# The first part of an attention-and-MoE kernel as one list of one-engine steps

## The chip, the cores and the metric

The kernel runs on one core of one Trainium2 chip. The metric is device time in microseconds (us), the median of several executions; one more execution is profiled. PE is the matmul engine (PEld its weight loads), DVE is VectorE, ACT is ScalarE, POOL is GpSimd, SP only issues DMAs.

## What is computed

```python
scores = scale * (q_c @ k_c.T)              # 8 batches, 8 heads, chunks of 64 tokens, head size 64
attn = softmax(scores)                      # max, exp, sum, divide
x = (attn @ v_c), laid out as 4608 tokens x 512
h = max(max(x @ w1, x @ w2), x @ w3)        # three 512 x 768 weights
x = h @ w_out                               # 768 x 512
h = maximum(x @ w_in2, 0) ; out = h * h @ w_out2    # 512 x 2048, 2048 x 512
```

q, k and v are float32; all weights arrive as float64.

## The kernel before, in words

Attention works on 36 tiles of 128 tokens; four tiles make a block of 512 tokens, so there are nine blocks. A matmul operand is kept as two float32r parts, a high part and the low rest, and every product is three matmuls (high-high, high-low, low-high) of 128x256.

A tile passes through S (scores, on PE), the row maximum and the subtraction (DVE, L277 and L280), the exponential (ACT, L281), the row sum and its reciprocal (DVE, L287 to L292), the product with the reciprocal (POOL, L293), T (transpose, PE), a copy out of PSUM (ACT, L303), X (the product with v, PE), the high part (ACT, L328) and the low part (DVE, L333).

A float64 weight tile of 128x512 is called a unit; there are 24 in the first part (w1, w2, w3 and w_out for each of six slices f of 128 hidden columns). `convert` turns one into its two parts: ACT takes the absolute value of the upper words and the scaled lower words (L98, L99), DVE rebuilds the exponent in three steps (L101, L103, L106), POOL adds the lower words (L112), ACT rounds to the high part (L113), POOL subtracts for the low part (L115). Raw tiles go through four buffers (`in`).

An item (b, f, w) is the projection of block b with weight w of slice f: 24 matmuls into one of two PSUM buffers (`p`). w = 0 is copied out by ACT (L375), w = 1 and w = 2 take the running maximum on DVE (L378, L382), and after w = 2 ACT and DVE make the two parts of h (L384, L386). `g2(b, f)` multiplies them by w_out, also 24 matmuls, into four accumulators. At the end of block 0 these are written out.

The first part runs under a manual schedule: each engine gets its instructions in the order in which the Python code emits them. It covers eight attention tiles (blocks 0 and 1), the 24 conversions, all 36 items of blocks 0 and 1, the products `g2` of block 0, and the scores and the transposes of tiles 8 and 9 and the scores of 10 and 11. A loop over the eight tiles interleaves attention, conversion and the first items; a second loop takes the other items, and a generator `flow` works off the conversions from unit 8 on, mostly one after the other. `heat(n)` emits n matmuls on zeros. After the first part come the products of block 1, the other blocks and the second MoE layer, whose code is not touched; they begin with X of tiles 8 and 9.

Of the kernel before, what the change touches and what calls it, by code (L numbers as in the profile page):

```python
# [2 lines left out]

# [38 lines left out]
def kernel(ctx: ExitStack, tc, qkv, w123, w_out, w_in2, w_out2, out):  # L42
# [48 lines left out]
    def convert(raw, hi, lo):  # L91

        w0, w1 = raw[:, :, 0], raw[:, :, 1]
        a = tmp("a")
        r = tmp("r")
        au, ru = a.bitcast(U32), r.bitcast(U32)
        v = nc.vector
        nc.scalar.activation(a, w1.bitcast(F32), AF.Abs)  # L98
        nc.scalar.activation(ru, w0, AF.Copy, scale=2.0**-29)  # L99
# [6 lines left out]
        v.scalar_tensor_tensor(out=au, in0=w1, scalar=0xC0000000, in1=au, op0=ALU.bitwise_and, op1=ALU.bitwise_or)  # L106
        if hi is None:
            for h, part in enumerate(lo):
                c = slice(h * HC, h * HC + HC)
                nc.gpsimd.tensor_tensor(out=part.bitcast(U32), in0=au[:, c], in1=ru[:, c], op=ALU.add)  # L110
            return
# [5 lines left out]
    def unit_steps(src, name, keep, late=False):  # L117
# [7 lines left out]
        if src.dtype == F32:  # L125
            raw = ap.tile([P, 512], F32, tag="in", name="raw", bufs=4)
            nc.sync.dma_start(raw, src)
            yield
            split(halved(raw), hi, lo)
        else:  # L130
            raw = ap.tile([P, 512, 2], U32, tag="in", name="raw", bufs=4)
            nc.sync.dma_start(raw.rearrange("p n w -> p (n w)"), src.bitcast(U32))
            yield
            yield from convert(raw, hi, lo)

# [37 lines left out]
    def park(n, g):  # L173
# [5 lines left out]
        for r in range(2):  # L179
            for a in range(2):  # L180
# [5 lines left out]
                else:  # L186
# [3 lines left out]
                    for k, _ in enumerate(convert(raw, None, parts)):  # L190
                        if k in (0, 2):
                            yield
# [81 lines left out]
    def att_M(t):  # L274
# [5 lines left out]
        nc.vector.tensor_tensor(out=e, in0=s, in1=mx.to_broadcast([P, H, D]), op=ALU.subtract)  # L280
        nc.scalar.activation(e, e, AF.Exp, scale=1.0 / D ** 0.5)  # L281
        e_t[t] = e

    def att_N(t):
# [21 lines left out]
    def att_V(*ts, tag="at"):  # L306
# [19 lines left out]
        for t in ts:  # L326
            o = t % 4
            nc.scalar.copy(x_t[t // 4][0][:, :, o * P:o * P + P], xps_t[t])  # L328
# [42 lines left out]
    def p1_end(b, f, w, p):  # L371
# [181 lines left out]
    for f in range(NF1):  # L553
        units += [w123_steps(f, w) for w in range(3)] + [wo_steps(f)]
# [16 lines left out]
    M = [att_M(t) for t in range(8)]  # L571
    N = [att_N(t) for t in range(8)]
    U = units
    none = iter(())

    heat(11)
    att_load(0)
    att_load(1)
    go(U[0])
    att_load(2)  # L580
    att_load_v(0)
    att_load_v(1)
    go(U[1])
    att_load(3)
    att_load_v(2)
    att_load(4)
    att_load_v(3)
    att_load_v(4)
    go(U[2])
    att_S(0)  # L590
    att_S(1)
    heat(4)
    go(M[0], M[0], U[0], M[1], N[0], M[1], N[0], N[0], U[0], U[0], U[0])
    att_S(2)
    heat(10)

    mid = {2: [(0, 0, 0)], 3: [(0, 0, 1)], 4: [(0, 0, 0)], 5: [(0, 0, 2)], 6: [(0, 1, 1)], 7: [(0, 1, 2)]}
    late = {4: [(0, 0, 1)], 5: [(0, 1, 0)], 6: [(1, 0, 0)], 7: [(0, 0)]}
    parts, ends = {}, []

    def chunk(w, halves):
        if len(w) == 2:
            return g2(*w)
        if w not in parts:
            parts[w] = proj(W123[w[1:]], x_t[w[0]], f"p{w[2]}", 2 if halves else 1)
        p = next(parts[w])
        if p is not None:
            ends.append(p1_end(*w, p))


    for k in range(8):
        u = U[k]
        m, n = (M + [none] * 2)[k + 2], (N + [none])[k + 1]
        if k:
            att_L(k - 1)
        att_T(k, "acc" if k < 7 else "at")
        if k < 2:
            heat(3)
        if k:
            go(m, u, m, u, u)  # L620
        else:
            go(m, m)
        for w in mid.get(k, ()):
            chunk(w, k < 4)
        att_V(k, tag="acc" if k < 7 else "at")
        if k < 5:
            att_S(k + 3)
        go(n, u, n, n, u)
        go(u)
        go(U[k + 1], U[k + 3])  # L630
        if k < 3:
            att_load(k + 5)
            att_load_v(k + 5)
        if k < 2:
            heat(4)
        for w in late.get(k, ()):
            chunk(w, w[0] == 1)
        for e in ends:
            run(e)
        ends.clear()  # L640
    att_L(7)
    for load in (att_load_v, att_load):
        for t in (8, 9):
            load(t)

    def flow(todo):

        for j, u in enumerate(todo):
            ahead = todo[j + 1:j + 4:2]
            for i in range(5):  # L650
                go(u)
                if i == 2:
                    go(*ahead[:1])
                if i == 4:
                    go(*ahead[1:])
                yield

    items = [(1, 0, w) for w in range(3)] + [(1, 1, w) for w in range(3)] + [(0, 1)]
    for f in range(2, NF1):
        for w in range(3):  # L660
            items += [(0, f, w), (1, f, w)]
            if w == 1 and f > 2:
                items.append((0, f - 1))
    items.append((0, NF1 - 1))
    conv = flow(U[8:])
    end = none
    att = steps(8, NT1)
    for i, it in enumerate(items):
        if i in (len(items) - 8, len(items) - 4, len(items) - 2):
            att.pop(0)()  # L670
        if len(it) == 2:
            g2(*it)
            continue
# [158 lines left out]
```

## Time and profile before

| | before |
|---|---|
| median of 3 runs | 1410.78 us (1410.49 to 1413.93) |
| the profiled execution | 1411.77 us, its span 1410.0 us |
| PE busy | 1375.9 us (98%) |
| DVE busy | 892.6 us (63%) |
| ACT busy | 521.0 us (37%) |
| POOL busy | 223.3 us (16%) |
| mean granted clock of PE | 0.995 |

The span runs from the first to the last instruction; the 1.8 us around it belong to every execution. Busy time is not progress: matmuls are pipelined, and matmuls on zeros count as busy too. The granted clock is 1.00 at 2.4 GHz and 0.50 at 1.2 GHz.

### The profile page before, as it was taken

Reading aid. Unit: us, or ns where it says so; the run is one execution under the profiler, and the core shown is the slowest. Engines: PE = TensorE matmul, PEld = TensorE weight load, DVE = VectorE, ACT = ScalarE, POOL = GpSimd, SP = SyncE. Lnnn points to the kernel's source line nnn. Section 1 sums busy time; section 2 is a strip of 40 time slices with the busy share of each in tenths; the row PEclk is TensorE's granted clock in tenths of the full one; section 3 lists DMA queues with packets and bytes.
Section 4 is the critical chain, followed back from the end, with each engine's and each line's share of the span. In section 5 each row is a group of like instructions: output and inputs, shape, how many; then the busy total and the mean of one; then the engine's idle time right before and its main releaser. Section 6 shows DMA issues by size and latency. Waiting matters only on the chain.

```text
span 1410.0 us, 32701 instructions
## 1 busy us (share of the span) xinstructions
PE 1375.9 (98%) x13719; PEld 1358.2 (96%) x13719; DVE 892.6 (63%) x1413; ACT 521.0 (37%) x904; POOL 223.3 (16%) x204
## 2 busy tenths in 40 slices
PE   7879999999999999999999999999999999999998
PEld 5779999999999999999999999999999999999998
DVE  6644446565666565633166666666667888778774
ACT  4443324333333343321133333333334444444442
POOL 3444313232424223300000000000000000000000
PEclk9999999999999999999999999999999999999999
DMA  9332244473645554535643333333498443344331
GB/s 280 95 106 84 81 151 136 144 246 106 225 165 165 195 195 136 206 109 182 193 151 142 143 142 136 144 140 136 164 348 324 144 149 121 124 146 141 129 135 46
DMA packets 101235, 222.33 MB, mean 158 GB/s; under 512 B 11232, under 2 KB 20448, under 8 KB 101088
## 3 DMA queue, kind: packets, MB, share of 16 engines
q1 hardware_dynamic: 101088, 220.25, 46.3%
q8 instruction: 107, 1.75, 0.5%
q14 instruction: 40, 0.33, 0.1%
HBM read 134.22 MB, written 85.98 MB: 156 GB/s over the span
## 4 chain that ended last, share of the span: by engine, by line
PE 85%; DVE 1%; issue 0%; POOLq 0%; POOL 0%; ACT 0%; DVEq 0%; ACTq 0%
PE o L492 25%; PE z L441 24%; PE p L347 24%; PE y L347 9%; PE X L322 1%; PE S L270 1%; PE T L299 1%; DVE pl L199 0%; DVE u L464 0%; POOL u L464 0%; POOLq L828 0%; DVE mx L277 0%; DVE sm L287 0%; DVE e L280 0%; DVE h L382 0%
## 5 line engine op out<-in xcount | busy, mean ns | idle before, releaser
L441 PE MATMUL z<-yxh,wih 128*128 128x256 f32 x560 | 154.9, 277 | 0.0
L441 PE MATMUL z<-yxh,wil 128*128 128x256 f32 x560 | 154.7, 276 | 0.0
L441 PE MATMUL z<-yxl,wih 128*128 128x256 f32 x560 | 154.7, 276 | 0.0
L492 PE MATMUL o<-wo2h,gl 128*128 128x256 f32 x504 | 140.7, 279 | 0.0
L492 PE MATMUL o<-wo2h,gh 128*128 128x256 f32 x504 | 140.4, 279 | 0.0
L492 PE MATMUL o<-wo2l,gh 128*128 128x256 f32 x504 | 140.2, 278 | 0.0
L492 PE MATMUL o<-wo2h,gxl 128*128 128x256 f32 x504 | 140.1, 278 | 0.0
L492 PE MATMUL o<-wo2h,gxh 128*128 128x256 f32 x504 | 139.9, 278 | 0.0
L492 PE MATMUL o<-wo2l,gxh 128*128 128x256 f32 x504 | 139.9, 278 | 0.0
L464 POOL TENSOR_TENSOR u<-u,s 128x512 f32<-128x512 f32 x9 | 11.7, 1296 | 761.6 <-DVE u L464 761.6
L464 DVE TENSOR_TENSOR c<-z,s 128x512 f32<-128x512 f32 x108 | 74.3, 688 | 89.4 <-PE z L441 84.8
L441 PE MATMUL z<-yh,wih 128*128 128x256 f32 x448 | 124.2, 277 | 0.0
L441 PE MATMUL z<-yh,wil 128*128 128x256 f32 x448 | 124.1, 277 | 0.0
L441 PE MATMUL z<-yl,wih 128*128 128x256 f32 x448 | 124.1, 277 | 0.0
L384 ACT CAST hh<-h 128x512 fp32r<-128x512 f32 x54 | 33.5, 621 | 241.3 <-DVE h L382 224.2
L382 DVE TENSOR_TENSOR h<-p,m 128x512 f32<-128x512 f32 x54 | 37.2, 688 | 133.7 <-PE p L347 132.8
L449 ACT COPY s<-z 128x512 f32<-128x512 f32 x108 | 63.3, 586 | 133.5 <-PE z L441 132.2
L441 PEld LDWEIGHTS z<-yxh,wih 128*128 128x128 f32 x560 | 105.2, 188 | 0.2 <-DVE c L464 0.2
L441 PEld LDWEIGHTS z<-yxh,wil 128*128 128x128 f32 x560 | 105.1, 188 | 0.0
L441 PEld LDWEIGHTS z<-yxl,wih 128*128 128x128 f32 x560 | 105.1, 188 | 0.0
L492 PEld LDWEIGHTS o<-wo2l,gh 128*128 128x128 f32 x504 | 94.9, 188 | 0.0
L492 PEld LDWEIGHTS o<-wo2h,gl 128*128 128x128 f32 x504 | 94.7, 188 | 0.0
(184 smaller groups left out, 4101.6 us busy)
## 6 DMA issues: line engine op xcount, KB each, us to landing
gd<-g SPq DMA_DIRECT2D x144, 256.0 KB, 2.0
gr<-gd SPq DMA_DIRECT2D x72, 512.0 KB, 4.1
qk<-in_qkv SPq DMA_DIRECT2D x28, 512.0 KB, 3.8
raw<-in_w_out SPq DMA_DIRECT2D x22, 512.0 KB, 3.5
raw<-in_w SPq DMA_DIRECT2D x18, 512.0 KB, 3.8
v<-in_qkv SPq DMA_DIRECT2D x72, 128.0 KB, 5.7
yd<-ys SPq DMA_DIRECT2D x36, 256.0 KB, 2.9
yr<-yd SPq DMA_DIRECT2D x18, 512.0 KB, 5.1
```

The source lines that it names most:

```text
L270: nc.tensor.matmul(s_t[t][o:o + D, h ^ t % 2, :], lhsT=q[r, h, :], rhs=k[r, h, :], start=True, stop=True,)
L299: nc.tensor.transpose(tp[:, p * P:(p + 1) * P], e[:, 2 * p:2 * p + 2, :].rearrange("p h k -> p (h k)"), ident)
L322: nc.tensor.matmul(xps_t[t][j * D:j * D + D, p, c * D:c * D + D], lhsT=v[o:o + D, c, p, :], rhs=et[o:o + D, p, q:q + D], start=True, stop= ...
L347: nc.tensor.matmul(dst[:, c], lhsT=lhs, rhs=rhs[:, c], start=first and i == 0 and j == 0, stop=last and j == len(pairs) - 1, skip_group_ch ...
L382: nc.vector.tensor_tensor(out=h, in0=p, in1=st[b], op=ALU.max)
L384: nc.scalar.copy(hh, h)
L441: nc.tensor.matmul(dst[:, a * HC:a * HC + HC], lhsT=l[:, a, w], rhs=r[:, k, :], start=first and a + k + j == 0, stop=j == 2, skip_group_ch ...
L449: nc.scalar.copy(t, bank[tag])
L464: (eng or nc.vector).tensor_tensor(out=t, in0=x, in1=y, op=ALU.add)
L492: nc.tensor.matmul(bank[i][:, m * HC:m * HC + HC], lhsT=l[:, a, t], rhs=r[:, a, :], start=g + m + a + j == 0, stop=g == NG - 1 and j == 2, ...
```

## The change

The two loops and `flow` are replaced by one list of tokens. Each token emits instructions for one engine only (S, T, V, p, y for PE; M, N, C, L, l for DVE; X, E, H, A, h for ACT; G, s for POOL; qk, v, U are loads), and the number is the tile, the unit, or block, slice and weight.

- M is maximum and subtraction, X the exponential, N sum and reciprocal, G the product with it, E the copy of T, V the matmuls of X, H and L the high and the low part of a tile.
- A, C, s, h, l are the steps of a unit: absolute value and lower words (ACT), three steps of the exponent (DVE), the addition (POOL), the high part (ACT), the low part (DVE).
- q000 and q001 are first halves (256 columns) of items (0,0,0) and (0,0,1), p000 and p001 their second halves; any other p is a whole item. ep is what follows an item first (ACT for w = 0, DVE otherwise), hh and hl are the two parts of h, y is `g2` of block 0, @ and ~ are steps of the attention of tiles 8 to 11.

In a unit, the high part is now rounded from the value before the addition, the addition goes into the tile r, which lies in the weight pool, and the low part r minus high is taken on DVE instead of POOL. The conversions are spread so that up to three are between A and l. Attention of tiles 0 to 7 stands first, with the first five units beside it. 19 matmuls on zeros are emitted instead of 39. All other work is the same, and the order of every engine from the end of the list on is as before. Units 0 to 23 are in the order w1, w2, w3 of slice 0, of slice 1, w_out of slices 0 and 1, and from then on w1, w2, w3, w_out slice by slice.

```diff
-        nc.gpsimd.tensor_tensor(out=au, in0=au, in1=ru, op=ALU.add)
-        nc.scalar.copy(hi, halved(a))
-        yield
-        nc.gpsimd.tensor_tensor(out=lo, in0=halved(a), in1=hi.bitcast(F32), op=ALU.subtract)
...
+        def A():
+            if double:
+                box["r"] = wp.tile([P, 512], F32, tag="w", name="r")
+                box["a"] = rounded(raw, box["r"])
...
+        def s():
+            if double:
+                r = box["r"].bitcast(U32)
+                nc.gpsimd.tensor_tensor(out=r, in0=box["a"].bitcast(U32), in1=r, op=ALU.add)
+        def h():
+            nc.scalar.copy(hi, halved(box["a"]))
+        def l():
+            nc.vector.tensor_tensor(out=lo, in0=halved(box["r"]), in1=hi.bitcast(F32), op=ALU.subtract)
+        return {"A": A, "C": C, "s": s, "h": h, "l": l}
...
+    def tile_steps(k):
+        att_load(k)
+        yield
+        att_S(k, tag="acc")
+        yield
+        m, n = att_M(k), att_N(k)
+        for _ in range(2):
+            next(m)
+        yield
+        next(m, None)
+        yield
+        for _ in range(3):
+            next(n)
+        yield
+        next(n, None)
...
+    def item_steps(b, f, w):
+        for p in proj(W123[f, w], x_t[b], f"p{w}", 2 if (b, f, w) in split_items else 1):
+            yield
+        yield from p1_end(b, f, w, p)
+    tiles = [tile_steps(k) for k in range(8)]
+    items, split_items = {}, [(0, 0, 0), (0, 0, 1)]
...
+    order = """
+        qk0 qk1 v0 v1 U0 qk2 S0 v2 M0 S1 qk3 X0 v3 M1 N0 X1 U1 N1 A0 G0 U2 G1 T0 C0 S2 E0 qk4 s0
+        h0 V0 M2 v4 T1 H0 l0 S3 E1 L0 X2 U3 V1 M3 H1 N2 qk5 X3 A1 L1 G2 v5 N3 q000 A2 C1 G3 qk6 T2
+        S4 E2 v6 C2 s1 h1 V2 M4 qk7 h2 s2 T3 H2 v7 U4 U5 U6 E3 L2 X4 V3 l1 A3 N4 S5 H3 l2 G4 q001
+        L3 M5 p000 C3 U7 X5 T4 ep000 S6 E4 N5 s3 h3 V4 M6 G5 S7 H4 l3 X6 T5 L4 p001 E5 N6 A4 M7 V5
+        G6 A5 T6 ep001 p002 C4 U8 H5 E6 X7 L5 s4 h4 N7 A6 V6 ep002 G7 A7 p010 l4 C5 U9 H6 hh00 L6
+        s5 h5 T7 C6 U10 ep010 p011 E7 A8 l5 s6 hl00 h6 C7 U11 V7 A9 p012 ep011 s7 l6 H7 C8 U12 h7
+        A10 y0 L7 s8 h8 ep012 l7 hh01 l8 A11 hl01 p100 C9 U13 C10 U14 s9 h9 A12 p101 l9 s10 ep100
+        C11 U15 h10 p102 ep101 h11 s11 l10 A13 C12 U16 p110 ep102 s12 h12 C13 U17 A14 hh10 l12 s13
+        h13 p111 l11 ep110 A15 C14 U18 A16 l13 s14 p112 ep111 h14 C15 U19 A17 l14 s15 h15 y1 ep112
+        C16 U20 hh11 A18 hl11 s16 h16 p020 C17 U21 A19 l16 s17 l15 h17 p120 C18 U22 ep020 A20 l17
+        s18 C19 U23 h18 p021 ep120 A21 l18 s19 C20 h19 p121 ep021 h20 s20 C21 A22 p022 l20 s21 h21
+        ep121 A23 l19 l21 C22 p122 ep022 h22 s22 C23 hh02 p030 ep122 h23 s23 hl02 hh12 l22 l23
+        p130 ep030 hl12 hl10 p031 ep130 p131 ep031 y2 ep131 p032 p132 ep032 hh03 hl03 p040 ep132
+        hh13 hl13 p140 ep040 p041 ep140 p141 ep041 y3 ep141 p042 p142 ep042 hh04 hl04 p050 ep142
+        hh14 hl14 @ p150 ep050 ~ p051 ep150 ~ p151 ep051 @ y4 ep151 p052 @ p152 ep052 hh05 hl05 ~
+        y5 ep152 hh15 hl15 ~
+    """.split()
...
+    for token in order:
+        if token == "@":
+            att.pop(0)()
+            continue
+        if token == "~":
+            soften()
+            continue
+        kind, n = token.rstrip("0123456789"), token.lstrip(ascii_letters)
+        if kind == "v":
+            att_load_v(int(n))
+        elif kind in ("qk", *"SMXNGTEVHL"):
+            go(tiles[int(n)])
+        elif kind == "U":
+            U[int(n)] = units[int(n)]()
+        elif kind in (*"ACshl",):
+            U[int(n)][kind]()
...
+        if token in ("S1", "V1"):
             heat(4)
...
-    for k in range(8):
-        u = U[k]
-        m, n = (M + [none] * 2)[k + 2], (N + [none])[k + 1]
-        if k:
-            att_L(k - 1)
-        att_T(k, "acc" if k < 7 else "at")
-        if k < 2:
-            heat(3)
-        if k:
-            go(m, u, m, u, u)
...
-        *_, p = parts[it] if it in parts else proj(W123[it[1:]], x_t[it[0]], f"p{it[2]}")
-        go(conv, conv, end, conv, end)
-        soften()
-        if i < 8:
-            go(conv)
-        end = p1_end(*it, p)
```

POOL, the first nine rows of work, before (e is a tile's exponentials, rs its reciprocals, a and r a unit's words, w1_0l the low part of w2 in slice 0):

```order
L293 TENSOR_TENSOR e_198<-e_198,rs_212 128x512
L112 TENSOR_TENSOR a_201<-a_201,r_202 128x512
L115 TENSOR_TENSOR w0_0l_120<-a_201,w0_0h_119 128x512
L293 TENSOR_TENSOR e_209<-e_209,rs_303 128x512
L112 TENSOR_TENSOR a_307<-a_307,r_308 128x512
L115 TENSOR_TENSOR w1_0l_134<-a_307,w1_0h_133 128x2x256
L293 TENSOR_TENSOR e_260<-e_260,rs_385 128x512
L112 TENSOR_TENSOR a_389<-a_389,r_390 128x512
L115 TENSOR_TENSOR w2_0l_155<-a_389,w2_0h_154 128x512
```

and now:

```order
L319 TENSOR_TENSOR e_155<-e_155,rs_192 128x512
L319 TENSOR_TENSOR e_188<-e_188,rs_202 128x512
L150 TENSOR_TENSOR r_205<-a_206,r_205 128x512
L319 TENSOR_TENSOR e_269<-e_269,rs_334 128x512
L319 TENSOR_TENSOR e_329<-e_329,rs_353 128x512
L150 TENSOR_TENSOR r_342<-a_343,r_342 128x512
L150 TENSOR_TENSOR r_369<-a_370,r_369 128x512
L319 TENSOR_TENSOR e_432<-e_432,rs_489 128x512
L150 TENSOR_TENSOR r_483<-a_484,r_483 128x512
```

Each unit has left one of its two rows on POOL, the one that subtracts, and the first two tiles stand together.

DVE in the middle of the conversions, before: units w2 and w3 of slice 4 (raw tiles 1361 and 1404), with the ends of items of slices 2 and 3 (hl_1479, m1_1585) between them:

```order
L101 TENSOR_SCALAR a_1441<-a_1441 128x512
L386 TENSOR_TENSOR hl_1479<-h_1476,hh_1478 128x512
L103 TENSOR_SCALAR a_1441<-a_1441 128x512
L106 SCALAR_TENSOR_TENSOR a_1441<-raw_1361,a_1441 128x512
L101 TENSOR_SCALAR a_1512<-a_1512 128x512
L103 TENSOR_SCALAR a_1512<-a_1512 128x512
L106 SCALAR_TENSOR_TENSOR a_1512<-raw_1404,a_1512 128x512
L378 TENSOR_TENSOR m1_1585<-p1_1519,s1_1516 128x512
L101 TENSOR_SCALAR a_1580<-a_1580 128x512
L103 TENSOR_SCALAR a_1580<-a_1580 128x512
```

and now, from w3 of slice 4 (raw tile 1169) on, where p1_1350 is the item p021:

```order
L103 TENSOR_SCALAR a_1256<-a_1256 128x512
L105 TENSOR_SCALAR a_1256<-a_1256 128x512
L108 SCALAR_TENSOR_TENSOR a_1256<-raw_1169,a_1256 128x512
L156 TENSOR_TENSOR w1_4l_1121<-r_1212,w1_4h_1120 128x2x256
L103 TENSOR_SCALAR a_1295<-a_1295 128x512
L105 TENSOR_SCALAR a_1295<-a_1295 128x512
L108 SCALAR_TENSOR_TENSOR a_1295<-raw_1210,a_1295 128x512
L156 TENSOR_TENSOR w2_4l_1168<-r_1255,w2_4h_1167 128x512
L103 TENSOR_SCALAR a_1337<-a_1337 128x512
L105 TENSOR_SCALAR a_1337<-a_1337 128x512
L108 SCALAR_TENSOR_TENSOR a_1337<-raw_1252,a_1337 128x512
L413 TENSOR_TENSOR m1_1412<-p1_1350,s1_1334 128x512
```

A low part of an earlier unit stands between two conversions, and what ends an item waits behind them; three conversions now stand between two ends of items.

## Rows read from the trace of the kernel before

**Rows 1.** Stretches: length, busy of PE, PEld, DVE, ACT, POOL; clock, DMA share, GB/s.

```profile
0.00:187.70 187.70, 159.54 (x1792) 147.81 (x1792) 102.19 (x172) 73.33 (x128) 73.11 (x64) 0.96 0.44 130
...
187.70:1410.00 1222.30, 1216.31 (x11932) 1210.43 (x11928) 790.46 (x1242) 447.69 (x776) 150.22 (x140) 1.00 0.47 162
...
20.00:40.00 20.00, 12.39 (x244) 11.06 (x244) 16.95 (x29) 10.62 (x19) 10.62 (x9) 1.00 0.89 267
...
84.00:92.00 8.00, 2.95 (x14) 2.95 (x15) 3.88 (x7) 2.20 (x4) 3.68 (x3) 0.57 0.29 73
```

**Rows 2.** Waits of PE, 0 to 187.6 us: total us, times, longest us.

```profile
PE p L347 <- ACT s L375: 12.8, 5, 5.9
...
PE T L299 <- POOL e L293: 10.4, 6, 2.7
```

**Rows 3.** Waits of DVE, 0 to 187.6 us.

```profile
DVE a L101 <- ACT a L98: 22.8, 10, 2.8
```

**Rows 4.** The chain that ended last, in order of time: start us, us, what.

```profile
212.01 8.22 PE p L347 x72
```

**Rows 5.** Timeline of PE: start us, us, instruction [idle before it <-releaser].

```profile
25.51 0.66 PE L299 MATMUL T<-ident,e 128*128 128x128 f32 x4 [2.69 <-POOL e L293]
...
89.05 0.80 PE L347 MATMUL p<-xh,w_1h 128*128 128x256 f32 x2 [5.88 <-ACT s L375]
...
161.09 1.16 PE L270 MATMUL S<-qk 64*64 64x64 f32 x64
...
186.59 1.16 PE L322 MATMUL X<-et,v 64*64 64x64 f32 x64
```

**Rows 6.** Groups of DVE, 0 to 187 us: busy us, mean ns | idle before, releasers.

```profile
L378 DVE TENSOR_TENSOR m<-p,s 128x512 f32<-128x512 f32 x12 | 8.3, 689 | 16.2 <-PE p L347 9.5 <-ACT a L98 2.8 <-ACT s L375 2.4
...
L280 DVE TENSOR_TENSOR e<-S,mx 128x512 f32<-128x512 f32 x12 | 8.2, 685 | 0.2
...
L292 DVE RECIPROCAL rs<-sm 128x8 f32<-128x8 f32 x10 | 2.0, 203 | 0.8
```

**Rows 7.** Timeline of DVE, first conversion (start us, us).

```profile
7.43 0.69 DVE L277 TENSOR_REDUCE mx<-S 128x8 f32<-128x512 f32 x1 [6.30 <-PE S L270]
...
10.74 0.16 DVE L290 TENSOR_SCALAR sm<-sm 128x8 f32<-128x8 f32 x1
...
11.46 1.15 DVE L103 TENSOR_SCALAR a<-a 128x512 uint32<-128x512 uint32 x1
```

**Rows 8.** Timeline of DVE, a conversion with GpSimd idle.

```profile
83.14 0.69 DVE L386 TENSOR_TENSOR hl<-h,hh 128x512 fp32r<-128x512 f32 x1 [3.15 <-ACT hh L384]
...
83.75 0.42 DVE L101 TENSOR_SCALAR a<-a 128x512 f32<-128x512 f32 x1
...
84.21 0.43 DVE L103 TENSOR_SCALAR a<-a 128x512 uint32<-128x512 uint32 x1
...
84.67 0.69 DVE L106 SCALAR_TENSOR_TENSOR a<-raw,a 128x512 uint32<-128x512 uint32 x1
```

**Rows 9.** Timeline of DVE, three instructions beside work on GpSimd.

```profile
23.62 0.69 DVE L333 TENSOR_TENSOR xl<-X,xh 128x512 fp32r<-128x512 f32 x1 [0.83 <-ACT xh L328]
...
28.03 0.81 DVE L290 TENSOR_SCALAR sm<-sm 128x8 f32<-128x8 f32 x1
...
292.58 1.79 DVE L199 TENSOR_TENSOR pl<-s,ph 128x512 fp32r<-128x512 f32 x1
```

**Rows 10.** Timeline of POOL at the same moments.

```profile
11.29 1.04 POOL L293 TENSOR_TENSOR e<-e,rs 128x512 f32<-128x512 f32 x1 [9.99 <-DVE rs L292]
...
23.18 1.27 POOL L115 TENSOR_TENSOR w_0l<-a,w_0h 128x512 fp32r<-128x512 f32 x1 [0.73 <-ACT w_0h L113]
...
27.54 1.27 POOL L112 TENSOR_TENSOR a<-a,r 128x512 uint32<-128x512 uint32 x1 [2.09 <-DVE a L106]
...
292.06 1.75 POOL L148 TENSOR_TENSOR s<-q,q 128x512 f32<-128x512 f32 x1
...
293.77 1.75 POOL L148 TENSOR_TENSOR t<-q,q 128x512 f32<-128x512 f32 x1
```

More of the change, by code (lines that the diff above doesn't have):

```diff
@@ L2 @@
 from itertools import chain
+from string import ascii_letters
 import concourse.bass as bass
@@ L105, in convert, with unit @@
         yield
[L106 to L111, printed above, removed]
-        nc.gpsimd.tensor_tensor(out=au, in0=au, in1=ru, op=ALU.add)
-        nc.scalar.copy(hi, halved(a))
-        yield
-        nc.gpsimd.tensor_tensor(out=lo, in0=halved(a), in1=hi.bitcast(F32), op=ALU.subtract)
-    def unit_steps(src, name, keep, late=False):
+        v.scalar_tensor_tensor(out=au, in0=raw[:, :, 1], scalar=0xC0000000, in1=au,
+                               op0=ALU.bitwise_and, op1=ALU.bitwise_or)
+    def convert(raw, parts):
+        r = tmp("r")
+        a = rounded(raw, r)
+        yield
+        yield from rebuilt(raw, a)
+        au, ru = a.bitcast(U32), r.bitcast(U32)
+        for h, part in enumerate(parts):
+            c = slice(h * HC, h * HC + HC)
+            nc.gpsimd.tensor_tensor(out=part.bitcast(U32), in0=au[:, c], in1=ru[:, c], op=ALU.add)
+    def unit(src, name, keep, late):
         if late:
@@ L124, in unit_steps, with C @@
         keep(hi, lo)
-        if src.dtype == F32:
-            raw = ap.tile([P, 512], F32, tag="in", name="raw", bufs=4)
-            nc.sync.dma_start(raw, src)
[L128 to L134, printed above, removed]
+        double = src.dtype != F32
+        raw = ap.tile([P, 512, 2] if double else [P, 512], U32 if double else F32, tag="in", name="raw", bufs=4)
+        if double:
+            nc.sync.dma_start(raw.rearrange("p n w -> p (n w)"), src.bitcast(U32))
+        else:
+            nc.sync.dma_start(raw, src)
+        box = {"a": raw, "r": raw}
+        def A():
+            if double:
+                box["r"] = wp.tile([P, 512], F32, tag="w", name="r")
+                box["a"] = rounded(raw, box["r"])
+        def C():
+            if double:
+                run(rebuilt(raw, box["a"]))
+        def s():
+            if double:
+                r = box["r"].bitcast(U32)
[5 more added lines that the diff above has]
+        return {"A": A, "C": C, "s": s, "h": h, "l": l}
     def combine(q, left, eng):
@@ L189, in park @@
                     yield
-                    for k, _ in enumerate(convert(raw, None, parts)):
+                    for k, _ in enumerate(convert(raw, parts)):
                         if k in (0, 2):
@@ L326, in att_V, with att_H @@
         for t in ts:
-            o = t % 4
-            nc.scalar.copy(x_t[t // 4][0][:, :, o * P:o * P + P], xps_t[t])
+            if t >= 8:
+                att_H(t)
+    def att_H(t):
+        o = t % 4
+        nc.scalar.copy(x_t[t // 4][0][:, :, o * P:o * P + P], xps_t[t])
     def att_L(t):
@@ L553 @@
     for f in range(NF1):
-        units += [w123_steps(f, w) for w in range(3)] + [wo_steps(f)]
+        units += [lambda f=f, w=w: w123_unit(f, w) for w in range(3)] + [lambda f=f: wo_unit(f)]
     units[3:7] = units[4:7] + units[3:4]
@@ L570 @@
     warm = ps_tile("acc", "warm")
[L571 to L574, printed above, removed]
-    heat(11)
[L577 to L608, printed above, removed]
@@ L641 @@
[L641 to L663, printed above, removed]
@@ L680 @@
-    run(end)
-    soften()
-    run(conv)
+    U = {}
+    def tile_steps(k):
[8 more added lines that the diff above has]
+        next(m, None)
+        yield
+        for _ in range(3):
+            next(n)
+        yield
+        next(n, None)
+        yield
+        tp = att_T(k, "at")
+        yield
+        att_E(k, tp)
+        yield
+        att_V(k, tag="acc")
+        yield
+        att_H(k)
+        yield
+        att_L(k)
+        yield
@@ new lines @@
+    """.split()
+    att = steps(8, NT1)
+    heat(11)
+    for token in order:
[14 more added lines that the diff above has]
+            U[int(n)][kind]()
+        elif kind == "y":
+            g2(0, int(n))
+        else:
+            b, f, w = map(int, (n + "2")[:3])
+            if kind == "q" or kind == "p" and (b, f, w) not in items:
+                items[b, f, w] = item_steps(b, f, w)
+            go(items[b, f, w])
+        if token in ("S1", "V1"):
+            heat(4)
+        if token == "y3":
+            for load in (att_load_v, att_load):
+                for t in (8, 9):
+                    load(t)
```

57 lines of the change are left out of this document (19 added, 38 removed).

## The prediction

> **What bounds the kernel now.** I read the stretches first. From 187.7 us to the end PE is busy 1216.3 of 1222.3 us at clock 1.00; in the first 187.7 us it is busy 159.5, at 0.96, and part of that is zeros [rows 1]. So the time after the first part is PE's own work, and the change, which leaves that work and its order as they are, can only move the instant at which it begins. I take as that instant X of tiles 8 and 9, at 186.6 us [rows 5]. From there to the end of the span it is 1410.0 - 186.6 = 1223.4 us, which I keep.
>
> Then the waits of PE in the first part: 12.8 us in five waits for ACT's copy L375, 10.4 us in six for POOL's product L293 [rows 2]. The second is the chain of one attention tile, the first a conversion that is late: the copy stands on ACT behind the unit's steps. DVE itself waits 22.8 us, ten times, for a unit's absolute value from ACT [rows 3], one unit being worked through after the other. No engine but PE is full; the first part is a matter of order.
>
> **What the change removes.** The chain of one unit gets shorter (the high part no longer waits for POOL's addition), the next unit's ACT step stands ahead of need, and the eight tiles run two or three abreast. Twenty matmuls on zeros go; PE had time for them, so I count nothing for it. What is left must then be the work of the busiest engine. The question is which engine that is and how much of its work stands ahead of which item.
>
> **DVE's work, counted.** An item needs one of two PSUM buffers, so it waits for the end of the item two before it. The last of the items that stand on DVE behind conversions is p022: its ep022 stands behind C22, and p030 waits for it. After that one conversion and a few low parts are left, and PE has work without waiting. Up to ep022 the list puts on DVE:
> - 8 M. Maximum 0.69, subtraction 0.69 [rows 6, 7]; with what follows starting 0.08 early, as L101 at 83.75 starts 0.08 before the instruction of 83.14 ends [rows 8], 1.33 us each: 10.6.
> - 8 N. 0.69 for the sum, 0.16 and 0.20 for the two small steps [rows 6, 7]: 1.03 each, 8.2.
> - 23 C. From 83.75 to 84.67 + 0.69 it is 1.61 with GpSimd idle [rows 8], less 0.08: 1.53 each, 35.2.
> - 44 single instructions (8 L, 22 l, 3 hl, 11 ep) of 0.69 [rows 6, 8], 0.61 from start to start: 26.8.
>
> That is 80.8 us. The low parts on DVE are 13.4 of it; before, that work was POOL's.
>
> **What POOL adds to it.** Some DVE instructions stand still while POOL works. L290, 0.16 us alone [rows 7], took 0.81 beside the addition of 27.54 [rows 9, 10]. L103, 0.43 alone [rows 8], took 1.15 beside the product of 11.29 [rows 7, 10]. An instruction that reads PSUM did not stand still: 0.69 beside the subtraction of 23.18 [rows 9, 10]. And the kind of instruction that l is, two operands in SBUF, does it too: L199, otherwise 0.69, took 1.79 and POOL's 1.75 each where both engines had work [rows 9, 10]; they take turns, one turn in 1.71 us (292.06 to 293.77), so DVE loses 1.1 a turn.
>
> Each s begins when its C ends. What stands behind that C on DVE decides:
> - one instruction that does not mind, then one that does, which costs about 0.65 (0.81 - 0.16): N1, N5, l6, l10, C6, C13, C21, seven times, 4.6; two milder ones (N7, l4), 0.7;
> - two that mind, where s gets its turn after the first: C2, C10, C11, C17, C19, C20, hl00, l11, l15, nine times 1.1, 9.9;
> - C0 and C1 behind G1 and G3, as in the row at 11.46, 0.72 each: 1.5;
> - one that minds, one that does not, one that minds: C15, C16, l19, three times 0.55 (half of 1.1): 1.6.
>
> Behind C0, C2, C8 and G2, G4, G5, G6 stands enough that reads PSUM; nothing there. Together 18.3 us.
>
> The Trainium skill bears on this (SBUF — State Buffer, section "SBUF: two separate sides"): it says that the port pair shared by DVE and GpSimd is an exclusive lock, taken by DVE when it reads two SBUF operands or runs a two-port mode, and that the loser waits out the whole instruction. By whole instructions a turn would be 0.69 + 1.30, some 2.0 us, and the nine turns would cost 2.3 us more; the trace's 1.71 shows them overlapping a little. I keep the trace's number.
>
> **The sum.** DVE begins at 7.4 us [rows 7], as before, since S0 and the zeros ahead of it stay. 7.4 + 80.8 + 18.3 = 106.5 us for the end of ep022. Is PE there earlier? It can begin p000 after L3, behind 20.7 us of DVE work and 3.3 of the above, at 31.4. From p000 to p030 it has two half items (p000, p001) and 18 whole ones, y0 and y1 among them, at 2.74 each (72 matmuls in 8.22 us [rows 4]), 52.1, and attention: T of four tiles at 0.66, S of two and X of four at 1.1 (the rows show 1.16 for two tiles side by side; I take as much for one) [rows 5], 9.2. That is 61.3, so it would come to p030 at 93. DVE is 14 us later and decides. From p030 on 22 items and y's, 60.3 us, and S, T, S of tiles 8 to 11, 1.1 + 0.9 + 1.1 (T of two tiles lies between 0.66 and twice that) [rows 5]: 63.4. X of tiles 8 and 9 then begins at 106.5 + 63.4 = 169.9 instead of 186.6, 16.7 us earlier.
>
> The profiled execution took 1411.8 us for its span of 1410.0, so 1395.1; the median of the runs shown is 1.0 below it, 1410.8: I predict **1394 us**. POOL has 8 x 1.04 + 22 x 1.27 = 36 us of work up to there, and ACT in the whole first part about what it has now, 73 us [rows 1, 10]; neither decides.
>
> **The rivals.**
> - *l does not mind POOL.* Then only C and the small step of N wait: C2 and C10 1.1, C0 and C1 0.72, N7 0.3, and N1, N5, C6, C11, C13, C17, C19, C20, C21 0.65, together 9.8 instead of 18.3. X at 161.4, the time 1386 us. Against it stand the rows at 292.06; for it, that the turns there are with both queues full, while POOL here has pauses.
> - *Conversions late.* There are four raw buffers as before, and loading, ACT and DVE are queues that go in order. If a C still waits for its A as ten do now, 2.3 us each [rows 3], four such cost 9 us, 1403; at seven the gain is gone, and the change would not do what it says. In the first 40 us the loads are dense (267 GB/s from 20 to 40 us [rows 1]); against it, A now stands two or three units ahead.
> - *PE slow (the other side).* After a wait of 5.88 us PE's clock was 0.57 in the stretch from 84 to 92; after 2.69 us at 25.51 it stayed 1.00 [rows 1, 5]. With 20 matmuls on zeros fewer PE has pauses of some 3 us until p000. If it stayed at 1.2 GHz from p000 to p030, the 61.3 us would be 122.6: p030 at 154, X at 217.4, 1442 us. It decides against the change once about half of that work runs slow (p030 after 123.2, which is 186.6 - 63.4). The Trainium skill (TensorE: Matmul & The Clock Gate, Part 1) says that the throttled state is the default and that steady work lifts it; by it each long pause costs a while at half speed, as the row at 89.05 agrees. Falls of that kind before p030 mostly hide in the 14 us that PE has to spare, so I count none.
>
> **How the numbers follow.** Forecast (1389 to 1399): 0.53. l does not mind: 0.20. Conversions late but a gain: 0.20, reaching no gain in another 0.04. PE slow: 0.03. The range takes both neighbours, 1385 to 1402, and leaves out the last two and the tails of the neighbours, together 0.19. What a measurement of this kernel can tell from no change is 0.3%, 4.2 us: faster 0.93, same 0.03, slower 0.04.
>
> **What would show it.** Right: PE's first wait-free stretch begins with p030 at about 106 us and X of tiles 8 and 9 stands at about 170; DVE busy some 95% from 8 to 106 us; L103, L105 and L156 of after (C's first two steps and l) mean well above 0.42, 0.43 and 0.69; PE's long waits are for DVE's ep021 and ep022. Wrong: PE waiting for ACT's copies or for a load; PE at 0.5 for long; POOL's s far above 1.3 us; or waits after X that were not there before.

## The result, and the profile after

The kernel takes 1397.14 us (median of four, 1396.75 to 1397.70) against 1410.63 (four, 1410.47 to 1413.93): ratio 0.9899, 95% interval 0.9882 to 0.9916. It is 13.5 us faster; 1394 was forecast, in a range of 1385 to 1402. The profiled execution took 1396.79 us with a span of 1395.0.

The sum of the prediction beside what the trace shows:

| | predicted | measured |
|---|---|---|
| DVE begins | 7.4 | 6.2 |
| DVE waits for other engines up to ep022 | 0 | 2.1 |
| DVE's work up to ep022 | 80.8 | 80.8 |
| its standing still beside POOL | 18.3 | 18.7 |
| ep022 ends | 106.5 | 107.8 |
| from there to X of tiles 8 and 9 | 63.4 | 64.5 |
| X begins | 169.9 | 172.4 |
| from X to the end of the span | 1223.4 | 1222.6 |

The 18.7 are added up over the instructions (timeline of DVE), each with what it took above its duration alone; 80.8 is what is left of the 99.5 us in which DVE waited for nobody.

The timeline of PE at the places that the prediction speaks of, as in [rows 5] (start us, us, instruction [idle before it <-releaser]):

```profile
90.85 0.50 PE L382 MATMUL p<-xh,w_2h 128*128 128x256 f32 x2 [2.05 <-ACT s L410]
...
100.54 0.51 PE L382 MATMUL p<-xh,w_2h 128*128 128x256 f32 x2 [2.83 <-DVE m L413]
...
107.89 0.50 PE L382 MATMUL p<-xh,w_3h 128*128 128x256 f32 x2 [0.83 <-DVE h L417]
...
172.37 1.16 PE L353 MATMUL X<-et,v 64*64 64x64 f32 x64
```

The third row is p030; it waits for ep022 (L417), as forecast, and from there to X PE waits no more. The second waits for ep021. The first waits for ACT's copy, but ACT itself stood behind DVE. Timeline of ACT just ahead of it:

```profile
89.70 0.62 ACT L153 CAST w_4h<-a 128x512 fp32r<-128x512 f32 x1 [1.23 <-DVE a L108]
90.22 0.58 ACT L410 COPY s<-p 128x512 f32<-128x512 f32 x1
```

The copy stands on ACT behind a rounding that waited for a unit's third step on DVE. So all three waits come from one engine. Its share is in the stretches (columns as in [rows 1]):

```profile
8.00:107.90 99.90, 81.75 (x989) 76.01 (x984) 95.64 (x152) 59.84 (x106) 39.66 (x31) 0.98 0.64 190
60.00:107.90 47.90, 38.87 (x319) 37.22 (x317) 46.94 (x68) 27.31 (x48) 19.66 (x15) 1.00 0.54 165
```

DVE is busy 95.6 of 99.9 us (96%) up to p030, and 46.9 of 47.9 in the second half; PE has 9 us to spare there, and its clock is at its upper level. What DVE waited for up to ep022 (waits of DVE, 0 to 108 us: total us, times, longest us):

```profile
DVE mx L299 <- PE S L292: 7.0, 3, 5.1
...
DVE xl L368 <- ACT xh L363: 0.2, 1, 0.2
```

The longest of the first line lies ahead of its first instruction; the other 1.9 us are two scores that came late, and no C waited for its A, where before ten did [rows 3]. What standing still looks like (timelines of DVE, then of POOL):

```profile
6.22 0.69 DVE L299 TENSOR_REDUCE mx<-S 128x8 f32<-128x512 f32 x1 [5.09 <-PE S L292]
...
52.17 1.76 DVE L422 TENSOR_TENSOR hl<-h,hh 128x512 fp32r<-128x512 f32 x1
...
90.18 1.77 DVE L156 TENSOR_TENSOR wo3l<-r,wo3h 128x512 fp32r<-128x512 f32 x1
...
94.00 1.50 DVE L103 TENSOR_SCALAR a<-a 128x512 f32<-128x512 f32 x1
...
107.15 0.68 DVE L417 TENSOR_TENSOR h<-p,m 128x512 f32<-128x512 f32 x1
```

```profile
51.82 1.56 POOL L150 TENSOR_TENSOR r<-a,r 128x512 uint32<-128x512 uint32 x1 [1.65 <-DVE a L108]
...
89.90 1.50 POOL L150 TENSOR_TENSOR r<-a,r 128x512 uint32<-128x512 uint32 x1 [1.70 <-DVE a L108]
93.70 1.51 POOL L150 TENSOR_TENSOR r<-a,r 128x512 uint32<-128x512 uint32 x1 [2.29 <-issue]
```

The two subtractions at 52.17 and 90.18, 0.69 us alone, take 1.76 and 1.77 beside POOL's addition, as L199 did in [rows 9]; L103 at 94.00, 0.42 alone, takes 1.50. The groups of DVE up to 108 us, as in [rows 6], give the same by kind:

```profile
L103 DVE TENSOR_SCALAR a<-a 128x512 f32<-128x512 f32 x24 | 18.7, 777 | 0.0
...
L105 DVE TENSOR_SCALAR a<-a 128x512 uint32<-128x512 uint32 x23 | 13.2, 576 | 0.8
...
L422 DVE TENSOR_TENSOR hl<-h,hh 128x512 fp32r<-128x512 f32 x3 | 3.1, 1043 | 0.0
L156 DVE TENSOR_TENSOR w_2l<-r,w_2h 128x512 fp32r<-128x512 f32 x3 | 2.9, 953 | 0.0
...
L314 DVE TENSOR_SCALAR sm<-sm 128x8 f32<-128x8 f32 x8 | 2.6, 329 | 0.3
```

Against their durations alone (0.42, 0.43, 0.69, 0.69, 0.16) these five lose 7.9, 3.3, 1.0, 0.8 and 1.3 us up to ep022 (the 24th of the first line, at 107.75, stands behind ep022); the other 4.4 of the 18.7 are in the other low parts. Token by token the losses lie at the 23 places that the prediction names, from 0.15 at N7 to 1.11 at C17, and at one more, l7, with 0.26.

### The profile page after: what moved, and what is told of

The parts are those of the page before. It is cut to its first block, busy times and chain, and to the rows that moved or that the text cites. A ratio compares the mean times of both kernels' runs of the same rounds, so it can differ in the third digit from the quotient of the medians.

```text
span 1395.0 us, 32661 instructions
## 1 busy us (share of the span) xinstructions
PE 1369.1 (98%) x13699; PEld 1354.3 (97%) x13699; DVE 914.6 (66%) x1437; ACT 521.8 (37%) x904; POOL 195.1 (14%) x180
## 3 DMA queue, kind: packets, MB, share of 16 engines
q1 hardware_dynamic: 101088, 220.25, 46.9%
## 4 chain that ended last, share of the span: by engine, by line
PE 86%; DVE 1%; issue 0%; POOLq 0%; POOL 0%; ACT 0%; DVEq 0%; ACTq 0%
PE o L528 25%; PE z L477 25%; PE p L382 25%; PE y L382 9%; PE X L353 1%; PE S L292 1%; PE T L325 1%; DVE pl L219 0%; DVE u L500 0%; POOL u L500 0%; POOLq L844 0%; DVE mx L299 0%; DVE sm L311 0%; DVE e L302 0%; DVE h L417 0%
## 5 line engine op out<-in xcount | busy, mean ns | idle before, releaser
L417 DVE TENSOR_TENSOR h<-p,m 128x512 f32<-128x512 f32 x54 | 37.1, 688 | 132.0 <-PE p L382 131.1
```

## The experiments

Each edit stands against the kernel named with it. Time is the median; the ratio is to the kernel before, whose own median lay between 1410.5 and 1411.6 in the four groups of runs, so differences of about 1 us between runs of different groups are not told apart.

### What sets the end of the new kernel

**The low part back on POOL** (e1, from the changed kernel).

```diff
-            nc.vector.tensor_tensor(out=lo, in0=halved(box["r"]), in1=hi.bitcast(F32), op=ALU.subtract)
+            nc.gpsimd.tensor_tensor(out=lo, in0=halved(box["r"]), in1=hi.bitcast(F32), op=ALU.subtract)
```

> The changed kernel with one part undone: the low part of a unit is taken on GpSimd again, at its place in the list. Theory (DVE sets the first part up to ep022, and POOL's two-operand work and DVE's take turns): DVE gives away 22 x 0.61 = 13.4 us, but POOL gets 22 x 1.27 = 28 us of work that takes turns with DVE's conversions; about 0.3 us a unit are lost from unit 8 on and some more before, X of tiles 8 and 9 at 176 to 180 us instead of 172.4, the time 1402 (1398 to 1406). Rival (no turns for such work, DVE only relieved): ep022 moves 13 us forward, PE decides, the time 1386 to 1389.

1403.90 us, ratio 0.9945 (0.9930 to 0.9959): 6.8 slower, as the theory has it. Timeline of DVE:

```profile
92.62 1.37 DVE L105 TENSOR_SCALAR a<-a 128x512 uint32<-128x512 uint32 x1
...
95.08 1.38 DVE L105 TENSOR_SCALAR a<-a 128x512 uint32<-128x512 uint32 x1
96.49 1.66 DVE L108 SCALAR_TENSOR_TENSOR a<-raw,a 128x512 uint32<-128x512 uint32 x1
```

DVE has 0.69 us less to do in a unit and still loses: now the second and the third step of a conversion come to stand beside POOL's work too, and 0.43 and 0.69 become 1.4 and 1.7 there.

**The addition on DVE** (e3, from the changed kernel).

```diff
-                nc.gpsimd.tensor_tensor(out=r, in0=box["a"].bitcast(U32), in1=r, op=ALU.add)
+                nc.vector.scalar_tensor_tensor(out=r, in0=box["a"].bitcast(U32), scalar=0xFFFFFFFF, in1=r,
+                                               op0=ALU.bitwise_and, op1=ALU.bitwise_or)
```

> The changed kernel with a unit's addition on DVE instead of POOL (lower three bits joined by OR instead of added, so a carry is left out). Theory (turns with POOL cost DVE 16.6 of its 18.7 us at the additions, the other 2.1 at G): DVE gets 22 x 0.61 = 13.4 us more and loses 16.6 us of standing still, ep022 about 3 us earlier, the time 1394 (1392 to 1396), and POOL is nearly empty. Rival (DVE's work alone counts, the turns are hidden by waits it would have anyway): 13 us slower, 1410.

1394.19 us, ratio 0.9877 (0.9862 to 0.9892); X at 169.25. With 0.61 us more work a unit DVE is 3 us earlier: an addition on POOL costs DVE more than an addition on DVE. (An OR leaves out a carry; this run, e5 and e12 measure the time and are not replacements for the addition.)

**The addition folded into the second and third step** (e5, from the changed kernel; no POOL work in a unit, no instruction more on DVE).

```diff
-                run(rebuilt(raw, box["a"]))
+                a, r = box["a"], box["r"]
+                au, v = a.bitcast(U32), nc.vector
+                v.tensor_scalar(out=a, in0=a, scalar1=E_INF, scalar2=E_ZERO, op0=ALU.min, op1=ALU.max)
+                v.scalar_tensor_tensor(out=au, in0=au, scalar=3, in1=r.bitcast(U32),
+                                       op0=ALU.logical_shift_left, op1=ALU.bitwise_or)
+                v.scalar_tensor_tensor(out=r.bitcast(U32), in0=raw[:, :, 1], scalar=0x3FFFFFFF, in1=au,
+                                       op0=ALU.bitwise_or, op1=ALU.bitwise_and)
+                box["a"] = r
```

> The changed kernel with a unit's addition folded into C (its second step shifts and joins the lower three bits by OR, a lost carry left out, its third step masks; this holds for weights under 2 in size): no s on POOL at all, three DVE steps as before, the second with two operands (0.69 instead of 0.43 us). Theory (DVE's work up to ep022 and its turns with POOL set the first part): against the run with the addition on DVE 22 x 0.61 = 13.4 us go and 23 x 0.26 = 6 come, 7 to 8 us earlier, ep022 at 97 us, PE at 93 just ahead of it; the time 1387 (1384 to 1390). Rival (PE's own chain from p000 on already decides once the turns are gone): no more than 2 us under the 1394.2 of the addition on DVE.

1387.56 us, ratio 0.9829 (0.9814 to 0.9844), 9.6 faster than the changed kernel and the fastest of all. First p030 in the timeline of PE, then the stretch up to it:

```profile
98.50 0.50 PE L387 MATMUL p<-xh,w_3h 128*128 128x256 f32 x2 [0.58 <-DVE h L422]
```

```profile
8.00:98.50 90.50, 80.51 (x995) 76.11 (x993) 86.14 (x154) 60.25 (x106) 8.63 (x8) 0.98 0.71 209
```

p030 still waits for DVE, now at 98.5 instead of 107.9. DVE is busy 86.1 us on the way instead of 95.6, though its second step reads two operands now (0.69 instead of 0.43 us, 23 times, 6.0 more). Without POOL's additions 9.5 + 6.0 = 15.5 of the 18.7 us of standing still are gone; POOL's products are left.

### What the list can do without

**Absolute value directly ahead of its conversion** (e2, from the changed kernel: each A token of the list is put in front of its C token; a piece of the list).

```diff
-        qk0 qk1 v0 v1 U0 qk2 S0 v2 M0 S1 qk3 X0 v3 M1 N0 X1 U1 N1 A0 G0 U2 G1 T0 C0 S2 E0 qk4 s0
+        qk0 qk1 v0 v1 U0 qk2 S0 v2 M0 S1 qk3 X0 v3 M1 N0 X1 U1 N1 G0 U2 G1 T0 A0 C0 S2 E0 qk4 s0
```

> The changed kernel with each A (absolute value and lower words, ACT) moved to the place directly before its C: no unit stands ahead any more, all else as it is. Theory (that A stands ahead is what keeps DVE fed): each C waits for its A, 1.3 us of ACT's work and what is queued on ACT ahead of it, 1.8 to 2.3 us, less what the turns with POOL cost in the same gap; 23 such waits of 1.2 us net give some 28 us, the time about 1425 (1415 to 1435), slower than the kernel before. Rival (A would be there in time anyway, the gain comes from the attention of two blocks at the start): at most 3 us, 1397 to 1400.

1397.93 us, ratio 0.9902 (0.9887 to 0.9916). The theory fell: it costs at most 1 us, where 28 were expected. Waits of DVE, 0 to 186 us:

```profile
DVE a L103 <- ACT a L95: 3.3, 5, 0.7
```

Five waits, 0.7 us at most. A token says only where ACT gets its instruction, not when it works; ACT has room (in the changed kernel it is busy 59.84 of 99.9 us), and with its instruction later in the list it still comes in time. So the run says that the place of A in the list is not what matters; it does not say that DVE could do without an A that is finished early.

**Without the half items** (e4: q000 and q001 leave the list, p000 and p001 become whole items; `split_items = []`) and **without eight of the 19 matmuls on zeros** (e6: `heat(4)` behind S1 and V1 goes), both from the changed kernel.

> The changed kernel without the two half products: q000 and q001 are left out, the items (0,0,0) and (0,0,1) are done whole at p000 and p001. Theory (PE has 10 us or more to spare until p030, DVE decides): 2.7 us of PE's work move to after L3 and are covered, the time 1397 (1396 to 1398). Rival (PE's chain from p000 on decides): 2.7 us slower, 1400.

> The changed kernel without the two groups of four matmuls on zeros behind S1 and V1; the first eleven stay. Theory (PE has time to spare until p030, its clock does not matter there): 1397 (1396 to 1398.5). Rival (they keep the clock up, and PE at 1.2 GHz until p000 delays L3 and all behind it): 2 to 5 us slower.

1397.65 us (ratio 0.9903, 0.9886 to 0.9919) and 1397.20 us (0.9895, 0.9877 to 0.9913): neither costs anything that can be measured. In e6 PE's clock in the first 60 us is 0.91 instead of 0.97, and the time does not show it.

**One unit at a time** (e8, from the changed kernel: from unit 8 on the tokens A C s h l of a unit stand together, at the place of its l; a piece of the list).

```diff
-        C11 U15 h10 p102 ep101 h11 s11 l10 A13 C12 U16 p110 ep102 s12 h12 C13 U17 A14 hh10 l12 s13
+        A10 C10 U14 s10 h10 l10 p110 ep102 hh10 A12 C12 U15 s12 h12 l12 p111 A11 C11 U16 s11 h11
```

> The changed kernel with units 8 to 23 one after the other: A, C, s, h, l of a unit stand together where its l stands, the loads behind the conversions that free their buffers. Theory (units between A and l at the same time are what keeps DVE busy): a unit takes 1.3 + 1.5 + 1.3 + 0.7 us and three hops, about 5 instead of 3.1 us, as it did before; the second half of the gain goes, 8 to 12 us slower, 1405 to 1409. Rival (the gain comes from the attention at the start and the shorter chain alone): 1397 to 1400.

1411.46 us, ratio 1.0001 (0.9992 to 1.0011): the whole gain is gone, more than the theory's 8 to 12 us. Waits of PE and of DVE, 0 to 186 us:

```profile
PE p L382 <- ACT s L410: 11.5, 4, 4.7
PE p L382 <- DVE h L417: 5.0, 1, 5.0
```

```profile
DVE w_4l L156 <- POOL r L150: 4.8, 3, 1.9
```

DVE stands at each low part up to 1.9 us behind its own unit's addition, and what ends an item stands behind that. Yet one unit after the other does not cost 14 us in every order: e10 below works that way, and DVE stands at its low parts nearly as long (waits of DVE, 0 to 186 us):

```profile
DVE w_3l L115 <- POOL r L112: 4.5, 3, 1.5
```

It takes 1396.8 all the same, and its last conversion is later, not earlier. First step of the last conversion in the timeline of DVE, of e8 and then of e10:

```profile
126.67 0.42 DVE L103 TENSOR_SCALAR a<-a 128x512 f32<-128x512 f32 x1
```

```profile
140.48 0.42 DVE L101 TENSOR_SCALAR a<-a 128x512 f32<-128x512 f32 x1
```

e10 puts the last conversions among later items, the list puts nearly all of them ahead of p030. So e8 shows that this list needs several units at a time, and not that every order does.

### Where the gain over the kernel before comes from

In the kernel before, h stands behind s on two engines. ACT, in the wait of [rows 5] at 89.05 (timeline of ACT, kernel before):

```profile
82.51 0.60 ACT L384 CAST hh<-h 128x512 fp32r<-128x512 f32 x1
86.80 0.62 ACT L113 CAST wo2h<-a 128x512 fp32r<-128x512 f32 x1 [3.68 <-POOL a L112]
87.32 0.66 ACT L98 ACTIVATE a<-raw 128x512 f32<-128x512 f32 x1
...
88.44 0.56 ACT L375 COPY s<-p 128x512 f32<-128x512 f32 x1
```

It stands 3.68 us until POOL's addition is done, and the copy for which PE waits 5.88 us is behind it in its queue. So is the next unit's absolute value (87.32), for which DVE waits (timeline of DVE, kernel before; one of the ten waits of [rows 3]):

```profile
88.08 0.96 DVE L101 TENSOR_SCALAR a<-a 128x512 f32<-128x512 f32 x1 [2.72 <-ACT a L98]
```

The change takes this wait away inside a unit, and it also makes a new order. Five runs separate the two.

**The low part alone on DVE** (e7, from the kernel before).

```diff
-        nc.gpsimd.tensor_tensor(out=lo, in0=halved(a), in1=hi.bitcast(F32), op=ALU.subtract)
+        nc.vector.tensor_tensor(out=lo, in0=halved(a), in1=hi.bitcast(F32), op=ALU.subtract)
```

> The kernel before with one part of the change alone: the low part of a unit is taken on DVE instead of POOL, order and all else as before. Theory (there PE waits for conversions that are worked through one after the other; the low part in 0.69 instead of 1.29 us and a first step of the next unit that no longer waits for POOL shorten each by about 0.6 us): 3 to 6 us faster than before, 1405 to 1408. Rival (it only pays with the new order, or DVE's extra 15 us come to lie ahead of items): no change or slower, 1410 to 1414.

1410.68 us, ratio 0.9992 (0.9983 to 1.0002): nothing. Waits of DVE, 0 to 186 us:

```profile
DVE w_2l L115 <- ACT w_2h L113: 6.4, 3, 2.1
DVE w_3l L115 <- ACT w_3h L113: 6.4, 3, 2.1
```

DVE now stands some 2 us in front of each low part until addition and rounding are done, one after the other. The wait has only changed its place. Timeline of DVE, from the unit of the row at 83.75 [rows 8] on:

```profile
84.78 0.42 DVE L101 TENSOR_SCALAR a<-a 128x512 f32<-128x512 f32 x1
...
88.50 0.69 DVE L115 TENSOR_TENSOR wo2l<-a,wo2h 128x512 fp32r<-128x512 f32 x1 [2.11 <-ACT wo2h L113]
89.11 0.42 DVE L101 TENSOR_SCALAR a<-a 128x512 f32<-128x512 f32 x1
```

From one unit's first step to the next it is 4.33 us here, as before (83.75 to 88.08).

**The high part ahead and the low part on DVE** (e10, from the kernel before: a unit as the change makes it, in the old order).

```diff
-        nc.gpsimd.tensor_tensor(out=au, in0=au, in1=ru, op=ALU.add)
+        nc.gpsimd.tensor_tensor(out=ru, in0=au, in1=ru, op=ALU.add)
         nc.scalar.copy(hi, halved(a))
         yield
-        nc.gpsimd.tensor_tensor(out=lo, in0=halved(a), in1=hi.bitcast(F32), op=ALU.subtract)
+        nc.vector.tensor_tensor(out=lo, in0=halved(r), in1=hi.bitcast(F32), op=ALU.subtract)
```

> The kernel before with everything the change does inside a unit (high part from the value before the addition, low part on DVE), in the order of before. Theory (in the old order DVE stands still at each low part, 2 us behind POOL's addition and ACT's high part; with the shorter chain some 1.3 us): 0 to 4 us faster than before, 1407 to 1411; the order must bring the rest. Rival (the change inside a unit brings the gain, not the order): 1398 to 1402.

1396.82 us, ratio 0.9894 (0.9879 to 0.9909). The theory fell: the old order has the whole gain.

**The high part ahead alone** (e11: the same edit with `nc.gpsimd` left in the last line).

> The kernel before in its old order, with one thing of the change: the high part is rounded from the value before the addition, so ACT's rounding and POOL's addition start together; the low part stays on POOL, behind its addition. Theory (what the old order suffers from is ACT standing behind POOL's addition, with the copies of items queued behind it): PE's five waits for ACT's copies, 12.8 us, shrink to a few us, most of the 14 us comes, 1398 to 1402, X of tiles 8 and 9 at 173 to 178. Rival (both parts of the change inside a unit are needed, as the low part moved alone brought nothing): 1405 to 1411, X at 181 to 187.

1396.58 us, ratio 0.9896 (0.9879 to 0.9912); X at 171.43. The theory's mechanism is right, and it gives all, not most. Waits of PE, of ACT and of DVE, 0 to 186 us:

```profile
PE T L299 <- POOL e L293: 6.5, 6, 2.8
PE p L347 <- ACT s L375: 4.2, 2, 3.4
```

```profile
ACT w_2h L113 <- DVE a L106: 6.6, 3, 2.9
```

```profile
DVE a L101 <- ACT a L98: 10.1, 9, 1.3
```

PE's waits for ACT's copies go from five of 12.8 us to two of 4.2, those for POOL's product from 10.4 to 6.5 [rows 2]; together 12.5 of the 15.2 us by which X begins earlier. The rounding now waits for DVE's third step, and DVE's waits for the next unit's absolute value go from 22.8 us, 2.8 at most [rows 3], to 10.1, 1.3 at most.

**The high part behind the addition, in the new list** (e9, from the changed kernel; where h stands ahead of s in the list, it is put behind).

```diff
-            nc.scalar.copy(hi, halved(box["a"]))
+            nc.scalar.copy(hi, halved(box["r"]))
```

> The changed kernel with the longer chain of before inside a unit: the high part is rounded from the sum, so h waits for POOL's addition (h moved behind s in the list where it stood ahead). Theory (with several units between A and l the chain of one unit is covered): l stands later by 0.6 us after an addition that often comes late itself; some of the 23 low parts wait on DVE, 1 to 5 us, the time 1398 to 1402. Rival (the shorter chain is what makes the list work): DVE stands still some 1.3 us at most low parts, 15 us or more, 1410 and above.

1399.97 us, ratio 0.9918 (0.9901 to 0.9934): 2.8 slower. With other units' work in between, what costs 14 us in the old order costs 3 here. The time is the theory's, the place is not: no low part waits. PE's waits for ACT's copies grow (waits of PE, 0 to 186 us):

```profile
PE p L382 <- ACT s L410: 7.0, 4, 2.4
```

But DVE still sets the end, 3.6 us later (p030 in the timeline of PE, then waits of DVE, 0 to 112 us):

```profile
111.52 0.50 PE L382 MATMUL p<-xh,w_3h 128*128 128x256 f32 x2 [1.04 <-DVE h L417]
```

```profile
DVE mx L299 <- PE S L292: 8.7, 5, 6.0
DVE xl L368 <- ACT xh L363: 1.5, 2, 1.2
```

It begins 0.9 us later in this execution and waits 2.1 us more in the attention, for scores and for tiles' high parts, than in the changed kernel. How much of that comes from the edit is not shown.

**The folded addition in the old order** (e12, from the kernel before: the second and third step as in e5, the low part on DVE; a piece).

```diff
+            v.scalar_tensor_tensor(out=au, in0=au, scalar=3, in1=ru, op0=ALU.logical_shift_left, op1=ALU.bitwise_or)
+            yield
+            v.scalar_tensor_tensor(out=ru, in0=w1, scalar=0x3FFFFFFF, in1=au, op0=ALU.bitwise_or, op1=ALU.bitwise_and)
+            nc.scalar.copy(hi, halved(r))
+            yield
+            nc.vector.tensor_tensor(out=lo, in0=halved(r), in1=hi.bitcast(F32), op=ALU.subtract)
```

> The kernel before in its old order, with the units' addition folded into the exponent's second and third step as an OR (the value differs where the addition carries), and the low part on DVE: no POOL work in a unit. Beside it stands the same folding in the new list (1387.6). Theory (with POOL out of the way DVE's own order counts: in the old one its low part stands directly behind ACT's rounding, some 0.8 us a unit, and the next unit's first step behind its absolute value): 1391 to 1395, so the list is worth 3 to 7 us here. Rival (the list is worth nothing beside the shortened unit, as in the run of both parts in the old order, 1396.8 against 1397.1): 1386 to 1390.

1393.41 us, ratio 0.9876 (0.9861 to 0.9891), as the theory has it: the same unit takes 5.8 us less in the new list. A wait that is left in the old order (waits of DVE, 0 to 186 us):

```profile
DVE w_3l L109 <- ACT w_3h L107: 2.1, 3, 0.7
```

All runs of one kind together (median us):

| a unit's addition, high part, low part | old order | new list |
|---|---|---|
| POOL, behind, POOL | 1410.6 (before) | not run |
| POOL, behind, DVE | 1410.7 (e7) | 1400.0 (e9) |
| POOL, ahead, POOL | 1396.6 (e11) | 1403.9 (e1) |
| POOL, ahead, DVE | 1396.8 (e10) | 1397.1 (after) |
| folded, ahead, DVE | 1393.4 (e12) | 1387.6 (e5) |

Read along the rows, the list is worth 10.7 us where the high part stands behind the addition, loses 7.3 where the low part is POOL's, makes no difference in the unit of the change, and is worth 5.8 without additions on POOL. Down the columns, rounding ahead with the low part on DVE is worth 13.9 in the old order (e7 to e10) and 2.8 in the list.

## Why the prediction was right

**What the change moves** was right: the time behind X stays (1222.6 us against 1223.4), and PE waits only 0.6 us in all after p030.

**DVE sets the end**: shown. It is 96% busy up to ep022, PE waits for ep021 and ep022, and moving work to and from DVE's way moves the time (e1, e3, e5). PE had 9 us to spare between 60 and 107.9 us alone, so PE's own work of 93 us up to p030 is plausible; it was not measured by itself.

**The count**: 99.5 us of DVE work and standing still against 80.8 + 18.3 = 99.1. The places were right too, all 23, each within 0.3 us of its price, with one of 0.26 left out; and l does mind POOL (1.07 at l11, 1.08 at l15): the rival that it does not, 1386, is out. (The 2.3 us that the prediction puts on turns of whole instructions is 9 x 0.28 = 2.5; nothing rests on it.)

**What was mis-sized.** The prediction had DVE begin at 7.4 "as before, since S0 and the zeros ahead of it stay"; it began 1.2 earlier. That is not the list's doing. The eleven matmuls on zeros ahead of S0 were faster in this execution than in that of before (4.87 us) and in that of e3, which has the same list up to there (timeline of PE, after and then e3):

```profile
1.19 3.91 PE L596 MATMUL warm<-zero 128*128 128x512 bf16 x11 [1.19 <-DVE zero L77]
```

```profile
1.19 4.87 PE L597 MATMUL warm<-zero 128*128 128x512 bf16 x11 [1.19 <-DVE zero L77]
```

Why is not shown. The prediction counted no wait of DVE for other engines, and there were 2.1; 0.97 of them are for the second scores, whose load was not there yet, so the early begin was mostly lost again. From p030 to X it counted 63.4 and it took 64.5: S, T and S take 3.0 of it (3.1 counted), the 22 items and products 61.5, 2.80 us each where 2.74 was counted. Rest of the span -0.8. Together -1.2 + 2.1 + 0.4 + 1.1 - 0.8 = +1.6, so 1396.7 where 1395.1 was predicted for one execution (1396.8 was measured). The other 1.3 us up to the median lie in the two profiled executions: that of before was 1.0 above its median, that of after 0.3 below. Terms of either sign partly cancel here; the count of DVE's work and standing still does not need that.

**The rivals.** Conversions were not late: no C waited for its A. PE was not slow: clock 0.98 up to p030, and even 0.91 in the first 60 us costs nothing (e6).

**One sentence of the prediction did not hold**: that the gain comes from a shorter chain, the next unit's ACT step ahead of need, and the tiles two or three abreast. The first alone gives all of it in the old order (e11). The place of the second in the list gives at most 1 us (e2). The third was not run by itself. The forecast of the time did not rest on this sentence: it adds up what the new kernel has to do, and leaves open what the old one loses. The new list brings nothing on top in the unit of the change: it trades PE's waits behind a chain for a full DVE, and both orders come out at 1397 by different limits. Why they meet there to within half a microsecond is not explained; the limits differ, as e12 and e5 show once POOL's addition is gone from both.

## What to carry to other kernels

When a change alters both the steps of a unit and their order, run each alone: here one operand (round before the addition, not after) gives the whole 14 us in the old order, the list gives 10.7 of them without it (e7 to e9), and the two do not add. Look for an engine whose queue stands behind another engine's step for a unit that nobody needs yet; what costs is the next thing in that queue, here a copy for PE and the next unit's first step for DVE. Once DVE is full, count what POOL does to it, instruction by instruction: an addition of 1.3 us on POOL cost DVE more than the same work on DVE (e3).

## What the runs showed of the hardware

The surprise is in e3: an addition that takes DVE 0.61 us from start to start costs it more when POOL does it. A waiting POOL instruction gets its turn even when DVE has work without a gap: at 89.90 POOL's addition starts behind the C that ended, lasts 1.50 instead of 1.27 [rows 10], and DVE's subtraction of 90.18 ends at 91.95, 1.1 later than alone.

The Trainium skill (SBUF — State Buffer, section "SBUF: two separate sides") says that the port pair of DVE and GpSimd goes to whoever starts first for a whole instruction. The trace agrees in direction, and 1.77 us is less than the 0.69 + 1.27 of two whole instructions by 0.2. The page names a second kind of instruction that needs the pair, one in a two-port mode. L103, with one operand and 0.42 us for as many columns as take others 0.69, takes 1.50 in the same place, which would fit; its mode is not in the trace. L417, which reads PSUM, takes its 0.68 throughout.
